# Last tokens as a ninth seven-product group, 64-key scores in 64x64 tiles, and new orders in a fused attention and gated-MLP kernel

## The chip, the cores and the metric

One core of a Trainium2 chip runs the kernel. The metric is the device time of one execution in microseconds; the comparison is between the kernel before and the kernel after the change, each run several times on the same chip. The engines are TensorE (PE, with its weight loads as PEld), VectorE (DVE), ScalarE (ACT), GpSimd (POOL) and SyncE (SP, which here only issues DMAs).

## The reference

Attention over 8 batch elements, 8 heads, 576 tokens and 64 features per head, with a bias that depends only on the distance of query and key, followed by a two-layer network with a sine gate on the 4608 tokens:

```python
scores = q @ k.T / 8 + bias_table[bucket(|i - j|)]        # T5 buckets, 32 of them
attn   = softmax(scores)
x      = (attn @ v), heads side by side                   # 4608 x 512
h      = x @ w_in                                         # 512 -> 2048
g      = h + sin(alpha * h)**2 / alpha
out    = g @ w_out                                        # 2048 -> 512, float32
```

## The kernel before

**Planning.** The kernel is a list of tasks with dependencies (`_graph`), each an emitting function of `_Ops` with an engine and a duration. `_Plan.run` walks through them with a small model of the chip; if `LINE` is given, the order of tasks on each engine is taken from that list of numbers and the model only gives start times, by which all engines' instructions are emitted. So the order of the work on PE, ACT, DVE, POOL and SP is written out, task by task, in `LINE`. `OPT` holds what else was chosen: which squares and copies run on ACT (`scalar`), which product pairs run in row halves (`rows`), the order of the POOL loads (`gq`).

**Attention.** Heads go in pairs (p = 0..3), one in each half of the 128 partitions. Keys lie on the output partitions of a score. `qk_t` (L1399, matmul L1405) scores 256 queries against 256 keys for a pair with four matmuls in two row halves of the array, 64 rows by 128 columns each; there are 16 such calls per element. `qk_tail` (L1385) takes the last 64 keys of two pairs against 512 queries, through `tail` (L1360): in the first two elements two 64x64 tiles on the diagonal (L1369), from the third element on one 128x128 matmul (L1364) with the block `kd`, in which `corners` (L1248, DVE) has put both heads' keys on the diagonal. `qk_s` (L1372) takes the last 64 keys against the last 64 queries in the same two ways, and `qk_r` (L1389, L1395) the first 512 keys against the last 64 queries. ACT takes the exponential of 1024 columns at a time (L1413, L1418), DVE multiplies the band near the diagonal by the exponentiated bias (L1441, L1423, L1427, L1383; the multipliers are `toep` and, made by POOL in `mask`, `mt`).

`av_w` (L1443) multiplies with v, for a pair p and a side w. For each group of 128 queries it issues one matmul of 130 columns for the last keys (L1451) and eight of 65 columns for the others (L1461); the 65th column gives the denominator. With w=0 there are two groups, with w=1 a third one for the last 64 queries, whose weights are 128 wide although 64 of the columns matter. `norm` (L1471, L1472) divides, and the result is turned either by PE and a copy (first element) or by a transposing DMA (`turn_x`) into `xT`, which holds four elements of 576 tokens.

**The network.** `moe_in` (L1498, matmul L1514) computes 128 rows of h for one block of tokens. The blocks `blk` are seven of 512 tokens, one of 448 and one of 576, cut where they cross the ring `xT` or a 512-column bank. Sine on ACT (`moe_sin`, L1522), square on ACT (L1527) or DVE (L1529), gate on DVE (`moe_g`, L1543).

The second layer works on groups of 512 tokens. For eight of them (`fast`) a 2x2 block product is made with seven block products instead of eight (`moe_fast`): `weight_sum` and `gate_sum` (L1578) make the sums on DVE, `products` (L1594, L1611) the products in 256-column matmuls into the PSUM banks X, Y and Z, `quarter` and `quarter_sum` (L1492/L1490, L1622) the results. Bank X holds products 1, 6, 7 and 4 in turn, each copied out before the next. The ninth group, the last 512 tokens, is multiplied directly: `moe_out` (L1547, L1558) with 512-column matmuls and `moe_half` (L1629, L1632) for its last 128 tokens.

**Row halves.** Changing how the array is divided costs PE time, so products may run "in rows": two products of a pair side by side, each on 64 rows of the contraction, first one half (turn 0), then, with halves swapped, the other (turn 1). `rows` names (pair number, f // 4). In `moe_fast` f // 4 is 0 or 1. Between the turns a DVE copy of one element of each bank (`touch_two`, L1587 and L1590) makes sure that both writes of a bank do not overlap.

**Loads.** q and k of the first elements come by POOL DMAs and are turned by PE (`turn`, L1340, on column halves of the array); later ones are staged in DRAM and turned by a transposing DMA. v comes by POOL DMAs (`load_v`, four per element, and `load_vt`, two per element for the last 64 keys). At the start `memsets` on DVE and `clear` on POOL write the constant parts.

Of the kernel before, what the change touches and what calls it, by code (L numbers as in the profile page):

```python
# [9 lines left out]
F16 = mybir.dt.float16  # L10
# [8 lines left out]
XR = 4 * S  # L19
# [82 lines left out]
class _Task:  # L102
    __slots__ = ("eng", "dur", "emit", "deps", "prio", "lat", "take", "seq", "sn", "name",
                 "m_in", "m_out", "pipe", "pkt", "flow", "start", "end", "idx", "got", "wait", "low", "alt",
                 "cold")

    def __init__(self, eng, dur, emit, deps=(), prio=0.0, lat=0.0, take=(), seq=None, name="",
                 mode=None, pipe=0.0, pkt=10, flow=False):
        self.pkt, self.flow = pkt, flow
        self.eng, self.dur, self.emit = eng, dur, emit  # L110
        self.deps = list(deps)
        self.prio, self.lat, self.take = prio, lat, list(take)
        self.seq, self.sn, self.name, self.pipe = seq, 0, name, pipe
        self.m_in, self.m_out = mode if isinstance(mode, tuple) else (mode, mode)
        self.start = self.end = None
        self.wait = 0.0
        self.low = 8
        self.cold = None
        self.alt = None
        self.got = []  # L120


class _Plan:
    HOP = 0.06
    LAT = {"PE": 0.17, "ACT": 0.1, "DVE": 0.09, "POOL": 0.1}
    SWITCH = {"PE": 0.096, "ACT": 1.3}
# [5 lines left out]
    STICK = 0.0  # L132

# [52 lines left out]
    def run(self):  # L186
# [21 lines left out]
        at = dict.fromkeys(line, 0)  # L208
        order = []
        while n:  # L210
            moved = False
            nxt = None
            for e, cand in pool.items():
# [4 lines left out]
                for t in cand:  # L218
# [6 lines left out]
                    for d in t.deps:  # L225
                        if d.eng != e or d.lat >= 1 or d.pipe:
                            x = d.end + self.HOP
                        else:
                            x = d.end + 0.025 if e == "DVE" else d.end - d.lat
                        if x > r:  # L230
                            r = x
                    r += t.wait
                    if t.pipe and e == "POOL" and len(self.segs[1]) >= self.OPEN:
# [50 lines left out]
                t.start = now  # L284
                free[e] = now + dur
# [1419 lines left out]
```

## Time and profile before

| | before |
|---|---|
| median of 3 runs | 373.88 us (373.77 to 374.48) |
| profiled execution: span | 370.6 us |
| instructions | 10525, of which 4379 matmuls and as many weight loads |
| busy PE, ACT, DVE, POOL | 356.4, 318.4, 318.8, 87.9 us |
| mean granted TensorE clock | 1.000 |

The span runs from the first to the last instruction of the profiled execution; the page gives no other time for that execution. A busy time is the time in which at least one instruction of the engine is in flight. For PE a matmul's own duration includes its drain, so the distance from one start to the next is what a matmul costs in a stream, not its duration. An idle time of an engine is put down to what ended it. In timeline rows the first column is the start, the second the time up to the end of the last instruction of the row; "x4" is the count; "64*128" is rows by columns of the array that are used.

### The profile page before, as it was taken

Reading aid. Unit: us, or ns where it says so; the run is one execution under the profiler, and the core shown is the slowest. Engines: PE = TensorE matmul, PEld = TensorE weight load, DVE = VectorE, ACT = ScalarE, POOL = GpSimd, SP = SyncE. Lnnn points to the kernel's source line nnn. Section 1 sums busy time; section 2 is a strip of 40 time slices with the busy share of each in tenths; the row PEclk is TensorE's granted clock in tenths of the full one; section 3 lists DMA queues with packets and bytes.
Section 4 is the critical chain, followed back from the end, with each engine's and each line's share of the span. In section 5 each row is a group of like instructions: output and inputs, shape, how many; then the busy total and the mean of one; then the engine's idle time right before and its main releaser. Section 6 shows DMA issues by size and latency. Waiting matters only on the chain.

```text
span 370.6 us, 10525 instructions
## 1 busy us (share of the span) xinstructions
PE 356.4 (96%) x4379; PEld 245.9 (66%) x4379; DVE 318.8 (86%) x711; ACT 318.4 (86%) x424; POOL 87.9 (24%) x105
## 2 busy tenths in 40 slices
PE   4969999999999999999999999999999999999996
PEld 3647546764666569755788987666965766745675
DVE  2679999999989998989998998899879997989733
ACT  5897999999999999999998999999899798476310
POOL 8895523085108000820050006200000000000000
PEclk9999999999999999999999999999999999999999
DMA  8999999899949954999799039907230012220014
GB/s 161 224 154 180 206 171 156 104 134 157 182 83 135 142 127 75 156 155 88 125 210 95 18 84 142 157 3 155 79 48 2 10 47 79 56 85 2 0 58 170
DMA packets 152415, 40.86 MB, mean 110 GB/s; under 512 B 134432, under 2 KB 151920, under 8 KB 152368
## 3 DMA queue, kind: packets, MB, share of 16 engines
q0 software_dynamic: 96656, 18.45, 60.2%
q1 hardware_dynamic: 55008, 21.22, 28.0%
q8 instruction: 34, 0.56, 0.6%
q10 hardware_dynamic: 704, 0.53, 0.6%
q14 instruction: 13, 0.11, 0.1%
HBM read 36.94 MB, written 15.93 MB: 143 GB/s over the span
## 4 chain that ended last, share of the span: by engine, by line
PE 87%; ACT 4%; POOL 3%; DMA 2%; DVE 2%; issue 1%; ACTq 0%; POOLq 0%; DVEq 0%
PE acc L1514 32%; PE acc L1611 26%; PE acc L1461 10%; PE acc L1405 9%; PE acc L1451 3%; PE acc L1558 3%; DMA wt<-in_k_dram 2%; PE acc L1364 2%; ACT s L1522 1%; PE acc L1395 1%; POOL mt L1292 1%; PE acc L1632 1%; DVE g L1543 1%; ACT u L1413 1%; POOL v L1219 1%
## 5 line engine op out<-in xcount | busy, mean ns | idle before, releaser
L1514 PE MATMUL acc<-xT,w_in 128*128 128x512 f16 (+3 forms) x704 | 134.2, 340 | 0.7 <-DVE g L1543 0.4
L1413 ACT ACTIVATE u<-acc 128x1024 f16<-128x1024 f32 x128 | 124.3, 1035 | 8.4 <-PE acc L1405 6.4
L1543 DVE SCALAR_TENSOR_TENSOR g<-s,inv_a,acc 128x512 f16<-128x512 f16 (+2 forms) x160 | 104.5, 691 | 8.6 <-ACT s L1527 6.5
L1522 ACT ACTIVATE s<-acc,alphaT 128x512 f16<-128x512 f32 (+2 forms) x144 | 93.2, 684 | 14.7 <-PE acc L1514 10.6
L1514 PEld LDWEIGHTS <-w_in 128*128 128x128 f16 x704 | 64.4, 98 | 55.8 <-DVE g L1543 1.8
L1611 PEld LDWEIGHTS <-g 128*128 128x128 f16 (+1 forms) x768 | 59.8, 96 | 18.0 <-issue 4.4
L1441 DVE TENSOR_TENSOR u<-u,toep 128x256 f16<-128x256 f16 (+1 forms) x128 | 59.4, 487 | 1.8 <-DMA toep<-e_sb 0.9
L1219 POOL DMA_DIRECT2D v<-in_v_dram x32 | 36.8, 1278 | 99.3 <-PE acc L1461 93.3
L1611 PE MATMUL acc<-w_out,g 128*128 128x256 f16 (+1 forms) x496 | 54.1, 271 | 0.0
L1405 PE MATMUL acc<-qT,kT 64*128 64x256 f16 x512 | 46.3, 279 | 3.9 <-DVE qT L1350 1.9
L1461 PE MATMUL acc<-v,u 128*128 128x65 f16 x1024 | 45.0, 193 | 0.1
L1527 ACT ACTIVATE s<-s 128x512 f16<-128x512 f16 (+2 forms) x67 | 41.4, 629 | 1.5
L1461 PEld LDWEIGHTS <-u 128*128 128x128 f16 x1024 | 40.6, 97 | 1.4 <-issue 0.5
L1611 PE MATMUL acc<-wt,g 128*128 128x256 f16 (+1 forms) x272 | 38.4, 272 | 0.0
L1611 PE MATMUL acc<-wt,sums 128*128 128x256 f16 (+1 forms) x272 | 34.6, 273 | 0.0
L1529 DVE TENSOR_TENSOR s<-s 128x512 f16<-128x512 f16 (+2 forms) x77 | 31.9, 422 | 2.6 <-ACT s L1522 2.3
L1472 DVE TENSOR_TENSOR xp<-acc,rden 128x256 f16<-128x256 f32 (+1 forms) x64 | 31.4, 491 | 2.2
L1405 PEld LDWEIGHTS <-kT 64*128 64x128 f16 x512 | 20.3, 96 | 16.1 <-issue 12.2
L1611 PEld LDWEIGHTS <-sums 128*128 128x128 f16 (+1 forms) x272 | 23.5, 97 | 7.9 <-issue 2.5
L1451 PE MATMUL acc<-vt,ut 128*128 128x130 f16 x128 | 28.3, 221 | 0.1
L1225 POOL DMA_DIRECT2D vt<-in_v_dram x16 | 14.1, 894 | 33.6 <-PE acc L1461 30.6
L1492 DVE COPY quarter<-acc 128x512 f32<-128x512 f32 x18 | 12.4, 687 | 9.3 <-PE acc L1611 4.7
(90 smaller groups left out, 361.6 us busy)
## 6 DMA issues: line engine op xcount, KB each, us to landing
out_dram<-quarter SPq DMA_DIRECT2D x32, 256.0 KB, 2.7
v<-in_v_dram POOLq DMA_DIRECT2D x32, 128.0 KB, 8.7
staged_k<-in_k_dram POOLq DMA_DIRECT2D x6, 576.0 KB, 10.8
staged_q<-in_q_dram POOLq DMA_DIRECT2D x5, 576.0 KB, 9.9
w_out<-in_moe_w_out_dram POOLq DMA_DIRECT2D x4, 512.0 KB, 8.7
w_in<-in_moe_w_in_dram POOLq DMA_DIRECT2D x4, 512.0 KB, 16.2
sums<-in_q_dram POOLq DMA_DIRECT2D x7, 144.0 KB, 5.6
out_dram<-outs SPq DMA_DIRECT2D x3, 256.0 KB, 2.0
```

Source lines behind the costliest of these rows:

```text
L1219: self.nc.gpsimd.dma_start(out=self.vs[t % 2][:, c, :, 0:D], in_=src)
L1405: self.nc.tensor.matmul(out=s[:, o:o + 256], lhsT=self.kT[t % 2][r, p, 128 * c:128 * c + 128], rhs=self.qT[t % 2][r, p, 256 * w:256 * w + ...
L1413: self.nc.scalar.activation(out=c["u"], in_=c["s"], func=AF.Exp, scale=0.125)
L1441: self.nc.vector.tensor_tensor(out=io, in0=io, in1=m, op=ALU.mult)
L1451: nc.tensor.matmul(out=c["av"][:, 130 * j:130 * j + 130], lhsT=tail, rhs=vt[:, p, :], start=True, stop=True, skip_group_check=True)
L1461: nc.tensor.matmul(out=c["av"][:, 130 * j + 65 * a:130 * j + 65 * a + 65], lhsT=l, rhs=vv[:, ch, 2 * p + a, 0:65], start=False, stop=True, ...
L1514: self.nc.tensor.matmul(out=c["h"][:, x:y], lhsT=self.w_in[:, j, 128 * f:128 * f + 128], rhs=self.xT[:, j, at:at + y - x], start=(j == 0 a ...
L1522: self.nc.scalar.activation(out=c["s"], in_=c["h"], func=AF.Sin, scale=self.alphaT[:, f:f + 1])
L1527: self.nc.scalar.activation(out=c["s"], in_=c["s"], func=AF.Square)
L1529: self.nc.vector.tensor_tensor(out=c["s"], in0=c["s"], in1=c["s"], op=ALU.mult)
L1543: self.nc.vector.scalar_tensor_tensor(out=o, in0=c["s"][:, x:y], scalar=self.inv_a[:, f:f + 1], in1=c["h"][:, x:y], op0=ALU.mult, op1=ALU.add)
L1611: self.nc.tensor.matmul(out=c[to][:, 256 * k:256 * k + 256], lhsT=a[r, 128 * k:128 * k + 128], rhs=b[r, :], start=to not in c["began"], st ...
```

## The change

What it does:

1. `blk` is nine blocks of 512. The last 64 tokens of all eight elements form a block of their own (`groups` number 8, the eighth in order, before the last element's 512). `xT` holds 512 tokens per element, a new `xt` all the tails. All nine groups go by seven products; `_blocks` of 448 and 576 tokens, `moe_out`, and `moe_half` are no longer used.
2. `av_w` makes two groups of 128 queries for either w; `av_tails` does the last 64 queries of all heads of an element in column halves of the array, `norm_tails` and `turn_tails` follow.
3. `tail` uses four 64x64 tiles for two head pairs in all elements; `kd`, `corners` and `clear` go; `load_vt` is four POOL DMAs per element; the constant memsets move to POOL.
4. `touch_two` goes. `half` lets PE wait for its own earlier matmul before the swapped half writes the bank. `rows` names 28 pieces.
5. The last group's product 3 gets a bank of its own (`W`), its product 4 is made and stored in two 256-column halves (`ending`).
6. New `LINE`, `scalar`, `gq` and rings (u tiles 14 for 12, x tiles 4 for 3); the model of the planner counts PE instructions and delays the start of a page of 256.

The diff, cut (the numbers of `LINE` and of `scalar` are left out):

```diff
-    blk=(512, 512, 512, 512, 512, 512, 512, 448, 576), fast=tuple(range(8)), split=True, no=2, nq=3, p_sum=0.1,
+    blk=(512, 512, 512, 512, 512, 512, 512, 512, 512),
+    groups=(0, 1, 2, 3, 4, 5, 6, 8, 7),
+    fast=(0, 1, 2, 3, 4, 5, 6, 7, 8),
...
-    rows=((0,2), (3,2), (4,2), (5,0), (5,1), (5,2), (5,3), (6,0), (6,1), (8,2), (9,0), (9,1),
-    (10,2), (11,2), (11,3), (12,2), (12,3), (13,0), (13,2), (15,0), (15,1), (15,2), (16,3),
-    (18,2), (20,3)), strict=False,
+    rows=((2, 0), (2, 1), (3, 0), (3, 1), (4, 0), (4, 1), (6, 0), (6, 1), (7, 0), (7, 1), (8,
+        0), (8, 1), (9, 0), (9, 1), (10, 0), (10, 1), (11, 1), (12, 0), (12, 1), (13, 1), (14, 0),
+        (14, 1), (15, 0), (15, 1), (16, 0), (16, 1), (18, 0), (18, 1)),
...
-    def tail(self, s, at, n, t, p, q0):
+    def tail(self, s, at, n, t, i, q0):
...
+        for b in range(2):
+            for a in range(2):
+                r, o = slice(64 * a, 64 * a + 64), 64 * (a ^ b)
+                self.nc.tensor.matmul(out=s[o:o + 64, 512 * b + at:512 * b + at + n],
+                                      lhsT=kT[r, 2 * i + b, 512:576], rhs=qT[r, 2 * i + b, q0:q0 + n],
+                                      start=True, stop=True)
...
+    def half(self, bank, at, n, lhsT, rhs, r, start):
+
+        was = None if start else self.wrote.get(bank)
+        if was is not None and was[0] != r and self.waited <= was[1]:
+            assert was[1] < self.marks, "no mark behind what the other half wrote"
+            hold = self.nc.tensor.nop(nofuse=True)
+            self.tc.add_manual_dep(hold.ins, self.at_mark[was[1]], SYNC, reason="rows")
+            self.waited = was[1] + 1
+        rows = slice(64 * r, 64 * r + 64)
+        self.last = self.nc.tensor.matmul(out=self.acc[:, bank, at:at + n], lhsT=lhsT[rows], rhs=rhs[rows],
+                                          start=start, stop=True, skip_group_check=True)
+        self.wrote[bank] = (r, self.marks)
...
+    def av_tails(self, c, bank, rs, t):
+
+        nc = self.nc
+        c["av"] = self.acc[:, bank, 0:260]
+        vv, vt, us = self.vs[t % 2], self.vt[t % 2], self.us[t % 2]
+        for i in range(2):
+            for b in range(2):
+                p, r = 2 * i + b, slice(64 * b, 64 * b + 64)
+                nc.tensor.matmul(out=c["av"][r, 130 * i:130 * i + 130], lhsT=us[:, 64 * p:64 * p + 64],
+                                 rhs=vt[:, p, :], start=not i, stop=True, skip_group_check=True)
+            for a in range(2):
+                for ch in range(4):
+                    for b in range(2):
+                        o, r = 512 * a + 256 * b + 64 * ch, slice(64 * b, 64 * b + 64)
+                        at = 130 * i + 65 * a
+                        nc.tensor.matmul(out=c["av"][r, at:at + 65], lhsT=rs[i]["u"][:, o:o + 64],
+                                         rhs=vv[:, ch, 4 * i + 2 * b + a, 0:65],
+                                         start=False, stop=True, skip_group_check=True)
...
-        T_v[t] += [gq(0.65, "load_vt", (t, a), deps=pre, pipe=0.27) for a in range(2)]
+        T_v[t] += [gq(0.6, "load_vt", (t, a, b), deps=pre, pipe=0.14) for a in range(2) for b in range(2)]
...
-        c22, q22 = finish(22, p7, zu, p5)
-        (p4, p3), all_c = group((4, 3), (ww(3), s_of(4)), ([c22], [q22]), ())
-        c12[1].deps.extend(p3)
-        finish(21, p4, None, [])
+        c22, q22, _ = finish(22, p7, zu, p5)
+        if i < 8:
+            (p4, p3), all_c = group((4, 3), (ww(3), s_of(4)), ([c22], [q22]), ())
+            c12[1].deps.extend(p3)
+            finish(21, p4, None, [])
+        else:
+            all_c = ending(cell, i, ww(3), s_of(4), c22, c12, xu)
...
+    def ending(cell, i, need4, need3, c22, c12, xu):
+
+        wu, p3 = [], []
+        for f in range(0, NF // 2, 2):
+            m = add("PE", 4 * 0.1092, None, prio=opt["p_mo"], mode="full", deps=need3(f) + p3[:1],
+                    name=f"mo{i}3.0.{f}", take=[] if p3 else [(1, wu)])
...
+        for k in range(2):
+            p4 = [add("PE", 4 * 0.1092, E("products", cell, i, (4,), f, 0, False, (k,), 4), prio=opt["p_mo"],
+                      mode="full", deps=need4(f) + [c22], name=f"mo{i}4.{k}.{f}") for f in range(0, NF // 2, 4)]
+            every += p4
+            cp = either(f"c21.{i}.{k}", 0.36, 0.38, lambda act, k=k: K.quarter_half(cell, k, act), deps=p4,
+                        prio=opt["p_ev"], take=[] if k else [(qr, ou)])
```

More of the change, by code (lines that the diff above doesn't have):

```diff
@@ L284, in run @@
                 t.start = now
+                if t.ins:
+                    for x in range(told // self.PAGE + 1, (told + t.ins) // self.PAGE + 1):
+                        pages.append(now + self.FETCH)
+                    told += t.ins
                 free[e] = now + dur
@@ L560, in later_loads @@
                     deps=[staged[t, kind]] + last_qk[t - 2])
-            if not kind:
-                e = add("DVE", 0.42, E("corners", t, range(NP)), deps=[c], prio=0.3)
-                e.wait = opt["late"]
-                T_c[t] = [e] * NP
             at[kind][t] = [c] * NP
@@ L748, in element @@
                     close(t, p, w, got)
+            if T_t[t] is None and all((t, x) in cells for x in (("R", 0), ("R", 1), ("S",))):
+                close_tails(t)
             yield
-        assert len(closed) == 2 * NP
+        assert len(closed) == 2 * NP and T_t[t] is not None
     BLK = _blocks(opt["blk"])
+    GROUPS = opt["groups"]
     NBLK = len(BLK)
@@ L838, in group @@
             turns = [[], []]
-            first = told = None
+            first = None
             for turn in range(2):
-                if turn:
-                    told = add("DVE", 0.18 if any(rows(f) for f in range(8)) else 0.0,
-                               lambda: any(rows(f) for f in range(8)) and K.touch_two(cell, names),
-                               deps=[m for m, r in turns[0] if r or opt["strict"]], prio=opt["p_touch"],
-                               name=f"told{pair}")
                 for f in range(0, NF // 2, 2):
@@ L937, in moe_out @@
                 break
-            if turn:
-                told = add("DVE", 0.12 if any(rows(f) for f in range(NF)) else 0.0,
-                           lambda: any(rows(f) for f in range(NF)) and K.touch(cell),
-                           deps=[m for m, r in turns[0] if r or opt["strict"]], prio=opt["p_touch"], name=f"told{pair}")
             for f in range(0, NF, 2):
@@ L1081 @@
+    n21 n22 n23 v2""".split(),)
 class _Ops:
@@ new lines, in full @@
+    def full(self, bank, at, n, lhsT, rhs, start):
+        if start:
+            self.wrote.pop(bank, None)
+        self.nc.tensor.matmul(out=self.acc[:, bank, at:at + n], lhsT=lhsT, rhs=rhs, start=start, stop=True,
+                              skip_group_check=True)
+    def half(self, bank, at, n, lhsT, rhs, r, start):
[9 more added lines that the diff above has]
+        self.wrote[bank] = (r, self.marks)
@@ L1441, in band_t, with av_w @@
         self.nc.vector.tensor_tensor(out=io, in0=io, in1=m, op=ALU.mult)
-    def av_w(self, c, bank, tiles, cr, ct, t, p, w):
+    def av_w(self, c, bank, tiles, ct, t, p, w):
         nc = self.nc
-        n = 3 if w else 2
-        c["av"] = self.acc[:, bank, 0:130 * n]
+        c["av"] = self.acc[:, bank, 0:260]
         vv, vt = self.vs[t % 2], self.vt[t % 2]
-        for j in range(n):
+        for j in range(2):
             o = 512 * (p % 2) + 256 * w + 128 * j
-            tail = ct["u"][:, o:o + 128] if j < 2 else self.us[t % 2][:, 64 * p:64 * p + 128]
-            nc.tensor.matmul(out=c["av"][:, 130 * j:130 * j + 130], lhsT=tail, rhs=vt[:, p, :],
-                             start=True, stop=True, skip_group_check=True)
+            nc.tensor.matmul(out=c["av"][:, 130 * j:130 * j + 130], lhsT=ct["u"][:, o:o + 128],
+                             rhs=vt[:, p, :], start=True, stop=True, skip_group_check=True)
@@ new lines, in turn_tails, with turn_tails_pe @@
+    def turn_tails(self, xcell, t):
+        self.nc.sync.dma_start_transpose(out=self.xt[:, t, :].rearrange("d (c s) -> d c s", c=2),
+                                         in_=xcell["x"][:, :])
+    def turn_tails_pe(self, xcell, cell, bank):
+        cell["o"] = o = self.acc[:, bank, :].bitcast(F16)
+        for i in range(2):
+            self.nc.tensor.transpose(out=o[:, 128 * i:128 * i + 128],
+                                     in_=xcell["x"][:, 128 * i:128 * i + 128], identity=self.ident[:, :])
@@ L1555, in moe_out @@
                     continue
-                r = slice(64 * (i ^ turn), 64 * (i ^ turn) + 64) if rows else slice(0, 128)
                 at = 128 * (tau % 4)
-                self.nc.tensor.matmul(out=c["mo"][i], lhsT=self.g[tau // 4][r, f, at:at + 128],
-                                      rhs=self.w_out[r, f, :], start=i not in c["began"],
-                                      stop=True, skip_group_check=True)
+                start = i not in c["began"]
                 c["began"].add(i)
+                args = (c["bank"][i], 0, DM, self.g[tau // 4][:, f, at:at + 128], self.w_out[:, f, :])
+                self.half(*args, i ^ turn, start) if rows else self.full(*args, start)
+        if rows and not turn:
+            self.mark()
     def weight_sum(self, i, k):
@@ L1608, in products @@
                         continue
-                    r = slice(64 * (x ^ turn), 64 * (x ^ turn) + 64) if rows else slice(0, 128)
-                    to, (a, b) = self.HOME[n], ab[n]
-                    self.nc.tensor.matmul(out=c[to][:, 256 * k:256 * k + 256],
-                                          lhsT=a[r, 128 * k:128 * k + 128], rhs=b[r, :],
-                                          start=to not in c["began"], stop=True, skip_group_check=True)
+                    to, (a, b) = "W" if n == 3 and "W" in c else self.HOME[n], ab[n]
+                    start = to not in c["began"]
                     c["began"].add(to)
+                    args = (c["bank"][to], 256 * k, 256, a[:, 128 * k:128 * k + 128], b)
+                    self.half(*args, x ^ turn, start) if rows else self.full(*args, start)
+        if rows and not turn:
+            self.mark()
     def quarter(self, c, what, act):
```

461 lines of the change are left out of this document (268 added, 193 removed), and 131 rows, old and new, of the table LINE.

## The prediction

> **What bounds it.** I read the page first (busy time, then the chain that ended last), then the busy time by stretches, then what TensorE waited for, then its timeline where the change bites.
>
> ```profile
> span 370.6 us, 10525 instructions
> PE 356.4 (96%) x4379; PEld 245.9 (66%) x4379; DVE 318.8 (86%) x711; ACT 318.4 (86%) x424; POOL 87.9 (24%) x105
> PE 87%; ACT 4%; POOL 3%; DMA 2%; DVE 2%; issue 1%; ACTq 0%; POOLq 0%; DVEq 0%
> 0.00:43.00 43.00, 32.71 (x624) 23.32 (x625) 30.27 (x84) 36.19 (x45) 34.51 (x56) 1.00 1.22 183
> 43.00:300.00 257.00, 256.70 (x3206) 178.59 (x3205) 237.34 (x523) 245.93 (x325) 53.36 (x49) 1.00 1.03 111
> 300.00:345.00 45.00, 44.48 (x375) 26.98 (x374) 39.37 (x85) 33.10 (x51) 0.00 (x0) 1.00 0.19 51
> 345.00:370.60 25.60, 22.46 (x179) 17.03 (x177) 11.80 (x22) 3.13 (x5) 0.00 (x0) 1.00 0.24 83
> ```
>
> The columns of the last four rows are the stretch, its length, then the busy time of PE, PEld, DVE, ACT and POOL. Three things are to be seen. From 43 us on PE is never out of work: 256.70 of 257 us, and the idle time at the end is the last copy and store. Second, 87% of the chain is PE's, so a microsecond of PE streaming taken out after 43 us is a microsecond of the kernel, as long as ACT and DVE keep up. Third, that condition is tight: in the long middle ACT is busy 245.93/257 = 95.7% and DVE 237.34/257 = 92.3%; only after 300 us have both room.
>
> The sum is made against this execution's span. The median of the runs shown, 373.88 us, lies 373.88 - 370.6 = 3.28 us above it; I hold that margin constant, so a microsecond of span is one of time. Less than 0.2% either way (0.75 us) counts as no change.
>
> **The 64-key scores in 64x64 tiles.** The 64 last keys of a head pair are scored at L1364 (from the third element on: a 128x128 block `kd` half zeros) and at L1369 (the first two elements: two 64x64 tiles).
>
> ```profile
> 273.45 0.59 PE L1364 MATMUL acc<-qT,kd 128*128 128x512 f16 x2
> 273.88 0.60 PE L1611 MATMUL acc<-wt,g 128*128 128x256 f16 x4
> 57.73 0.62 PE L1369 MATMUL acc<-qT,kT 64*64 64x512 f16 x4
> 58.28 1.48 PE L1611 MATMUL acc<-w_out,g 128*128 128x256 f16 x12
> 77.69 0.28 PE L1364 MATMUL acc<-qT,kd 128*128 128x64 f16 x4
> 77.80 0.60 PE L1611 MATMUL acc<-wt,sums 128*128 128x256 f16 x4
> ```
>
> Start to start is what counts (a row's own length includes its drain). Two full 512-column products take 273.88 - 273.45 = 0.43 us, 0.215 each. Four tiles on the diagonal take 0.55 us; less one change of mode (0.10, below) that is 0.45, two streams of 0.215, so tiles run two at a time. After the change the four matmuls of a call occupy four different quarters of the array. If all four run together, a call costs 0.215 instead of 0.43: 8 elements x 2 calls x 0.215 = **3.4 us** less. The last-query scores go from 0.11 (77.80 - 77.69) to about half: 8 x 0.05 = 0.4. Together **-3.8**. Bounds: -3.8 if four run at once; 0 if only pairs do, since four in pairs are again two streams. I take four, because the pieces are each in the trace: row halves side by side (next part) and column halves side by side (the transposes below).
>
> [...]
>
> **The last queries apart.** `av_w` for w=1 made three groups of nine matmuls, the third for 64 queries at a 128-wide price. It now makes two, and `av_tails` does all heads' last 64 queries of an element: 36 matmuls, in 18 pairs on the two column halves.
>
> ```profile
> 155.17 0.41 PE L1395 MATMUL acc<-qT,kT 64*128 64x64 f16 x16
> 155.41 0.38 PE L1405 MATMUL acc<-qT,kT 64*128 64x256 f16 x4
> 155.73 0.23 PE L1451 MATMUL acc<-vt,ut 128*128 128x130 f16 x1
> 155.80 0.41 PE L1461 MATMUL acc<-v,u 128*128 128x65 f16 x8
> 156.04 0.22 PE L1451 MATMUL acc<-vt,ut 128*128 128x130 f16 x1
> 156.09 0.41 PE L1461 MATMUL acc<-v,u 128*128 128x65 f16 x8
> 22.40 0.70 PE L1340 MATMUL acc<-ident,wt 96*64 96x96 f16 x24 [0.47 <-ACT u L1413]
> 23.03 0.31 PE L1369 MATMUL acc<-qT,kT 64*64 64x64 f16 x8
> ```
>
> A group of nine takes 156.04 - 155.73 = 0.31 (0.30 for the next, 33 ns a matmul). Removed: 32 x 0.30 = 9.6 us. The only column-tiled operation is the transposes: 24 in 0.63 us, less a mode change 0.53, 22 ns each or 44 a pair for 96 columns; two halves do run together. Added per element: 18 pairs at 33 ns = 0.60 (paced like the full groups) to 18 x 44 ns = 0.79 (paced like the transposes). I take 0.66, nearer the first because 65 columns stream in less than 96. 8 x 0.66 = 5.3. Net **-4.3** (-3.3 to -4.8).
>
> [...]
>
> **Output products and input matmuls.** The last 512 tokens took the direct way: at L1558 48 matmuls of 512 columns, at L1632 32 of 256.
>
> ```profile
> 341.03 0.86 PE acc L1558 x4
> 344.29 0.98 PE acc L1514 x8
> L1632 PE MATMUL acc<-w_out,g 128*128 128x256 f16 x32 | 4.5, 273 | 0.0
> L1514 PE MATMUL acc<-xT,w_in 128*128 128x512 f16 (+3 forms) x704 | 134.2, 340 | 0.7 <-DVE g L1543 0.4
> ```
>
> The chain gives 0.86/4 = 0.215 a 512-column matmul, so 48 x 0.215 + 32 x 0.109 = 13.8 us; seven products are 7 x 8 x 2 = 112 of 256 columns, 12.2. **-1.6**. Input: the same columns in 576 matmuls, not 704. Four of 576 columns in two pieces take 0.98, which is 0.215 x 576/512 x 4 = 0.97 and a hair: **-0.3**. Streaming in all: -3.8 - 4.3 - 1.6 - 0.3 = **-10.0 us**.
>
> **Mode changes.** 155.17 follows twelve 256-column products that started at 153.76 (12 x 0.109 = 1.31, so 155.07): a change full to row halves costs 0.10 us. In the timeline I count 162 such changes, 114 after 43 us, first and last:
>
> ```profile
> 57.42 0.38 PE L1514 MATMUL acc<-xT,w_in 128*128 128x512 f16 x1
> 57.73 0.62 PE L1369 MATMUL acc<-qT,kT 64*64 64x512 f16 x4
> 300.76 0.61 PE L1405 MATMUL acc<-qT,kT 64*128 64x256 f16 x8
> 301.30 0.93 PE L1514 MATMUL acc<-xT,w_in 128*128 128x448 f16 x4
> ```
>
> 110 of them enclose 55 visits to row halves. Seven of those visits hold products in row halves and gather about four scores each; the other 48 hold fewer than two. The `rows` list names 28 pieces instead of 9 that the code could use (entries with second number 2 or 3 never applied to products), so scores can be gathered behind products more often: I guess 55 visits become 35, -4.0 us (0 to -5.8, 26 left). Against it stand about 26 new visits: 12 for tails and 6 for last-query scores that used to be in full mode, 8 for `av_tails`, at 0.1 each where they touch another tiled visit and 0.2 where not: +2.6 to +5.2, taken 3.9. Net **0** (-3.2 to +5.2).
>
> **Waits.** The DVE touch between the two turns goes, and PE waits for its own earlier write instead.
>
> ```profile
> L1590 DVE COPY touched<-acc 1x1 f32<-1x1 f32 x6 | 0.6, 139 | 0.7 <-PE acc L1611 0.7
> L1587 DVE COPY touched<-acc 1x2 f32<-1x2 f32 x2 | 0.3, 144 | 0.3 <-PE acc L1611 0.3
> PE acc L1514 <- DVE g L1543: 0.4, 1, 0.4
> PE acc L1514 <- ACT u L1413: 0.2, 1, 0.2
> ```
>
> These are five pairs (three with two copies, two with one), and the only two PE waits after 43 us, in the last two rows, are for something else. Now 15 pairs have pieces in halves, each with one wait on PE's queue, behind which all matmuls stand, scores and so ACT's exponentials among them. A 256-column matmul lasts 273 ns where it streams 109, so an uncovered wait is about 0.17, a covered one nothing: 0 to 2.6, I take **+1.2**.
>
> **ACT and DVE.** Counted from the lists, 41 instead of 55 squares of the first seven blocks are ACT's: 14 x 0.632 = 8.8 us off ACT, 14 x 0.421 = 5.9 on DVE.
>
> ```profile
> L1527 ACT ACTIVATE s<-s 128x512 f16<-128x512 f16 x54 | 33.4, 632 | 1.1
> L1529 DVE TENSOR_TENSOR s<-s 128x512 f16<-128x512 f16 x58 | 23.9, 421 | 2.3 <-ACT s L1522 2.0
> L1254 DVE TENSOR_TENSOR kd<-kT 64x256 f16<-64x256 f16 x12 | 3.4, 284 | 0.4 <-DMA kT<-staged_k 0.3
> ```
>
> ACT's middle falls to 237; DVE's to 237.3 + 5.9 - 3.4 (corners) - 0.9 (touches) = 239. In a middle of about 250 us both are 95-96% busy, ACT as now, DVE tighter. Eight more gate sums (0.69 each) fall behind 300 us, where there is room. More than 250 to 240 can't be had. The last group's products share bank X through four copies; the third bank lets product 3 run under a copy (0.6-0.7 each). The front gets four small POOL loads of `vt` per element for two, while POOL is already 34.51 of 43 us busy there; DVE's memsets move onto POOL as `clear` leaves. Altogether new PE idle **+1.0** (-1 to +3); stores keep their last 256-column piece.
>
> **Sum:** -10.0 + 0 + 1.2 + 1.0 = -7.8: 373.9 - 7.8 = **366.1 us**.
>
> **Rivals.**
> *More gathered (12%).* All row visits merge and every wait is covered: -10.0 - 3.2 + 0 + 0.5 = -12.7, 361.2 us. For: the seven gathering visits. Against: ACT's 96%, which would leave it no slack.
> *ACT and DVE hold the middle, or tiles run in pairs only (20%).* If the middle doesn't get below 253, only 4 of its some 7 us are kept, and with the -1.6 and -0.3 behind 300 us and the waits the time is about 370. Pairs only: -7.8 + 3.8 = -4.0, 369.9. Against: both kinds of halves overlap in rows above. [...]
> *Nothing (4%).* Order gains and extra mode changes (+5.2), waits (2.6) and idle (2) cancel streaming: 373.7.
> *Slower: weight loads of the column halves don't overlap (9%).* Place: `av_tails`.
>
> ```profile
> L1340 PEld LDWEIGHTS <-sums 96*64 96x64 f16 x120 | 4.3, 142 | 2.1 <-issue 1.2 <-DMA sums<-in_k_dram 0.8
> L1340 PEld LDWEIGHTS <-wt 96*64 96x64 f16 x96 | 2.7, 116 | 1.5 <-issue 1.0 <-DMA wt<-in_q_dram 0.2
> L1461 PEld LDWEIGHTS <-u 128*128 128x128 f16 x1024 | 40.6, 97 | 1.4 <-issue 0.5
> ```
>
> A 64-wide load in column halves lasts 116 to 142 ns, 19 to 45 longer than a full one. If that came on top of each matmul's 33 ns, a visit would be 36 x 52 = 1.9 us, or with 78 ns 2.8, and eight of them 15.0 to 22.5 in place of 9.6: 366.1 + (15.0 - 5.3) = 375.8, up to 383. It decides from (5.3 + 7.8)/8 = 1.6 us a visit on. Against: with the very loads of 116 ns the transposes ran at 22 ns a matmul. [...]
>
> **Chances and range.** Forecast (363 to 369) 55%, the others as named: faster 0.87, same 0.04, slower 0.09. The range, 362 to 371, leaves out the best of the first rival and the slower ones.
>
> **What will show it.** L1364's successor: four 512-column tiles in about 0.22 us plus mode changes (0.43 refutes). A column-half visit of 36 in 0.60-0.79 us. Fewer than 114 mode changes after 43 us, or as many. PE idle in the middle under 2 us; ACT about 237 us of it. A wait of PE on itself beyond 0.2 us, or a middle over 254 us, would make the prediction wrong.

## The result, and the profile after

| | before | after |
|---|---|---|
| median | 374.18 us (4 runs, 373.77 to 374.52) | 367.69 us (4 runs, 367.27 to 368.35) |
| ratio | 1 | 0.9829, 95% interval 0.9813 to 0.9844 |
| profiled execution | 370.6 us span | 365.5 us span, 367.27 us time |

The forecast was 366.1 us in a range of 362 to 371. The kernel is faster by 6.5 us where 7.8 were expected.

The page of the kernel after, its span, busy times and shares of the chain:

```profile
span 365.5 us, 11027 instructions
...
PE 350.9 (96%) x4633; PEld 241.3 (66%) x4633; DVE 318.5 (87%) x694; ACT 311.2 (85%) x420; POOL 99.3 (27%) x139
...
PE 81%; DVE 7%; ACT 3%; DMA 3%; POOL 3%; issue 2%; POOLq 0%
```

The busy time by stretches of the same kernel (stretch, length, then PE, PEld, DVE, ACT, POOL, and the granted clock):

```profile
0.00:43.00 43.00, 34.83 (x609) 24.84 (x610) 28.47 (x73) 32.28 (x44) 32.99 (x72) 0.88 1.21 170
43.00:300.00 257.00, 254.22 (x3505) 172.61 (x3503) 236.21 (x523) 244.80 (x321) 63.82 (x64) 1.00 1.02 114
300.00:345.00 45.00, 45.00 (x376) 29.61 (x375) 40.41 (x81) 28.00 (x46) 0.62 (x1) 1.00 0.13 36
345.00:365.50 20.50, 16.87 (x149) 14.27 (x146) 13.38 (x21) 6.10 (x11) 1.82 (x3) 1.00 0.35 103
```

PE still sets the time, but 2.78 of the middle's 257 us are now idle, where it was 0.30 before: PE has begun to run into ACT and, once, into DVE. What it waited for, after 43 us (who, for whom: total us, times, longest):

```profile
PE acc L1520 <- ACT u L1535: 1.4, 4, 0.4
PE acc L1571 <- ACT u L1535: 0.5, 1, 0.5
PE acc L1478 <- ACT quarter L1643: 0.5, 1, 0.5
PE acc L1478 <- DVE quarter L1645: 0.2, 1, 0.2
```

Five waits are for an exponential (L1535), two for the copies of a quarter: one at 206.95 us (L1645), one in the last group at 361.74 us (L1643). PE's timeline of the changed kernel, where its new operations follow each other:

```profile
111.15 0.61 PE L1490 MATMUL acc<-wt,sums 64*128 64x256 f16 x8
111.70 0.41 PE L1470 MATMUL acc<-qT,kT 64*64 64x512 f16 x4
112.04 0.25 PE L1589 MATMUL acc<-vt,us 128*64 128x130 f16 x2
112.12 0.42 PE L1596 MATMUL acc<-v,ur 128*64 128x65 f16 x16
112.37 0.22 PE L1589 MATMUL acc<-vt,us 128*64 128x130 f16 x2
112.43 0.42 PE L1596 MATMUL acc<-v,ur 128*64 128x65 f16 x16
112.78 0.41 PE L1520 MATMUL acc<-qT,kT 64*128 64x64 f16 x16
...
222.99 0.63 PE L1470 MATMUL acc<-qT,kT 64*64 64x512 f16 x8
223.55 0.23 PE L1571 MATMUL acc<-vt,ut 128*128 128x130 f16 x1
```

Eight products in row halves stream 4 x 0.109 = 0.44 of the first 0.55 us; 0.11 is the change of mode behind them. The tile call takes 0.34 to the next start. Two calls in a row, at 222.99 us, take 0.56, so a call more costs 0.22, one stream of 512 columns, and the change behind it is the other 0.12. The visit of `av_tails`, 36 matmuls, takes 112.78 - 112.04 = 0.74, less a change 0.62.

### The profile page after: what moved, and what is told of

It reads as the page before. It is cut to its first block, busy times and chain, and to the rows that moved or that the text cites. A ratio compares the mean times of both kernels' runs of the same rounds, so it can differ in the third digit from the quotient of the medians.

```text
span 365.5 us, 11027 instructions
## 1 busy us (share of the span) xinstructions
PE 350.9 (96%) x4633; PEld 241.3 (66%) x4633; DVE 318.5 (87%) x694; ACT 311.2 (85%) x420; POOL 99.3 (27%) x139
## 4 chain that ended last, share of the span: by engine, by line
PE 81%; DVE 7%; ACT 3%; DMA 3%; POOL 3%; issue 2%; POOLq 0%
PE acc L1662 30%; PE acc L1478 15%; PE acc L1490 13%; PE acc L1576 9%; PE acc L1520 7%; PE acc L1571 3%; DVE g L1688 3%; DMA wt<-in_q_dram 2%; ACT u L1535 2%; PE acc L1470 2%; DMA wt<-in_k_dram 1%; DVE s L1674 1%; POOL sums L1330 1%; PE acc L1596 1%; DVE u L1563 1%
## 5 line engine op out<-in xcount | busy, mean ns | idle before, releaser
L1535 ACT ACTIVATE u<-acc 128x1024 f16<-128x1024 f32 x128 | 121.3, 1054 | 8.7 <-PE acc L1520 8.2
L1662 PE MATMUL acc<-xT,w_in 128*128 128x512 f16 x512 | 116.1, 379 | 0.0
L1667 ACT ACTIVATE s<-acc,alphaT 128x512 f16<-128x512 f32 x144 | 92.4, 684 | 19.5 <-PE acc L1662 18.5
L1688 DVE SCALAR_TENSOR_TENSOR g<-s,inv_a,acc 128x512 f16<-128x512 f16 x144 | 102.4, 743 | 2.8 <-ACT s L1672 1.4
L1563 DVE TENSOR_TENSOR u<-u,toep 128x1024 f16<-128x1024 f16 (+1 forms) x128 | 58.2, 487 | 2.6 <-DMA toep<-e_sb 1.2
L1520 PE MATMUL acc<-qT,kT 64*128 64x256 f16 (+1 forms) x768 | 55.2, 253 | 3.0 <-ACT u L1535 2.2
L1478 PEld LDWEIGHTS <-g 128*128 128x128 f16 x416 | 39.9, 98 | 14.1 <-issue 3.2
L1674 DVE TENSOR_TENSOR s<-s 128x512 f16<-128x512 f16 x83 | 33.7, 420 | 10.9 <-ACT s L1667 10.9
L1490 PE MATMUL acc<-w_out,g 64*128 64x256 f16 x496 | 41.0, 269 | 0.1
L1672 ACT ACTIVATE s<-s 128x512 f16<-128x512 f16 x61 | 37.1, 627 | 0.9
L1478 PE MATMUL acc<-wt,g 128*128 128x256 f16 x232 | 30.6, 273 | 0.7 <-ACT quarter L1643 0.5
```

Source lines behind the costliest of these rows:

```text
L1478: self.nc.tensor.matmul(out=self.acc[:, bank, at:at + n], lhsT=lhsT, rhs=rhs, start=start, stop=True, skip_group_check=True)
L1490: self.last = self.nc.tensor.matmul(out=self.acc[:, bank, at:at + n], lhsT=lhsT[rows], rhs=rhs[rows], start=start, stop=True, skip_group_c ...
L1520: self.nc.tensor.matmul(out=s[:, 512 * a + o:512 * a + o + n], lhsT=kT[r, p, 128 * c:128 * c + 128], rhs=qT[r, p, q0:q0 + n], start=True, ...
L1535: self.nc.scalar.activation(out=c["u"], in_=c["s"], func=AF.Exp, scale=0.125)
L1563: self.nc.vector.tensor_tensor(out=io, in0=io, in1=m, op=ALU.mult)
L1662: self.nc.tensor.matmul(out=c["h"], lhsT=self.w_in[:, j, 128 * f:128 * f + 128], rhs=x, start=j == 0, stop=j == 3, skip_group_check=True)
```

## The experiments

Times are medians; "over after" is the difference to 367.69 us, ratios are to the kernel before on the same chip.

**The kernel before again, unchanged, for a second trace.**

> The kernel before, unchanged, to see its own time beside its span. The prediction held the margin between the two at 3.28 us (373.88 - 370.6). The changed kernel shows 367.27 beside a span of 365.5, a margin of 1.77. Theory A: the margin is about 1.8 us in both kernels, and the profiled execution of before was one of some 372.4 us or its span was off; then spans of before come out near 372. Theory B: the margin of before really is about 3.3, so 1.4 of the 6.5 us gained lie outside the span.

374.18 us; ratio 1.000 (0.9988 to 1.0011). Its page, and its middle:

```profile
span 372.0 us, 10525 instructions
...
43.00:300.00 257.00, 256.41 (x3200) 177.96 (x3200) 237.38 (x524) 245.83 (x325) 53.28 (x49) 1.00 1.03 112
```

This execution took 374.17 us, 2.17 more than its span; for the kernel after it is 367.27 - 365.5 = 1.77. The span of 370.6 on which the prediction was built was a short one, so the margin of 3.28 was too large: other executions of this kernel with spans of 370.2 to 370.4 us took 372.3 to 372.6. With this trace the part from 43 us to PE's last matmul can be set out. Streaming is every matmul's columns at 0.417 ns and 2.3 ns more each, which is 0.216 us for 512 and 0.109 for 256 (the kernel after has 23 matmuls of 512 columns in 4.96 us from 334.73 us on, and 20 of 256 in 2.18 us from 332.33 us on); halves at one half and quarters at one quarter, but the tiles on the diagonal of the kernel before, which ran two at a time, at one half too. A change is taken at 0.105 us, between the 0.10 of the prediction's row and the 0.11 above; "rest" is what remains:

| 43 us to PE's end, us | before | after | difference |
|---|---|---|---|
| wall time | 325.92 | 319.34 | -6.6 |
| streaming | 309.4 | 296.7 | -12.6 |
| mode changes, 118 and 131 | 12.4 | 13.8 | +1.4 |
| PE waits | 0.6 | 2.6 | +2.0 |
| rest | 3.6 | 6.3 | +2.7 |

Over the whole run streaming falls by 10.6 us, from 328.8 to 318.2; the other 2.0 are done before 43 us now (1.1 against the first trace of before).

**Pairs in place of four tiles.** The second head's keys stay in the same column half as the first's, so that the four tiles of a call lie on the diagonal; such tiles took two streams before the change (0.45 us, as in the prediction).

```diff
-                r, o = slice(64 * a, 64 * a + 64), 64 * (a ^ b)
+                r, o = slice(64 * a, 64 * a + 64), 64 * a
```

(with the last keys' v, ones and multipliers laid out to match).

> The changed kernel with the four 64x64 tiles of a 64-key call on the diagonal only (both head pairs alike, with mask and v laid out to match), so that just two tiles can run at a time. Theory A (four at once): a visit of four 512-column tiles goes from 0.34 us back to 0.55, 16 x 0.215 + 8 x 0.05 = +3.8 us of PE, about 371.5, less what falls into the 2.6 us of PE idle. Rival B (tiles already run in pairs): no change, 367.7.

370.26 us, 2.6 over after; ratio 0.9896 (0.9879 to 0.9913). PE's timeline of this kernel at the same call:

```profile
112.65 0.62 PE L1470 MATMUL acc<-qT,kT 64*64 64x512 f16 x4
113.19 0.25 PE L1589 MATMUL acc<-vt,us 128*64 128x130 f16 x2
```

0.34 has become 0.54: one more stream of 512 columns, 0.20. Sixteen calls of 0.20 make 3.2 us and the last-query calls a few tenths. 2.6 us reach the time; about 1.0 falls in the front, before 43 us, where PE does not set the end. So four tiles do run at once, by 0.34 against 0.54. In the changed kernel the two row halves then write one bank at the same time, into different halves of its partitions (rows 0 to 63 into partitions 0 to 63 and rows 64 to 127 into 64 to 127, crosswise in the other bank).

**Column halves one after the other.** The loops of `av_tails` change order: all 18 matmuls of half 0, then those of half 1.

```diff
-        for i in range(2):
-            for b in range(2):
+        for b in range(2):
+            for i in range(2):
...
-            for a in range(2):
-                for ch in range(4):
-                    for b in range(2):
+                for a in range(2):
+                    for ch in range(4):
```

> The changed kernel with the 36 matmuls for the last 64 queries issued one column half after the other, instead of alternating. Theory A (the halves overlap, weight loads included): a visit goes from 0.64 us and a mode change to about 36 x 0.033 = 1.19, 8 x 0.55 = +4.4 us, about 372. Rival B (a visit is held by something the two halves share, the issue or the load of weights): a visit stays within 0.1 us and the kernel within 1 us. Rival C (a column half alone loads its weights slower than 33 ns a matmul): more than 1.3 us a visit.

371.48 us, 3.8 over after; ratio 0.9926 (0.9900 to 0.9952). First and last row of one visit, and the one behind it, in PE's timeline of this kernel:

```profile
73.50 0.24 PE L1589 MATMUL acc<-vt,us 128*64 128x130 f16 x1
...
74.42 0.41 PE L1595 MATMUL acc<-v,ur 128*64 128x65 f16 x8
74.77 0.25 PE L1470 MATMUL acc<-qT,kT 64*64 64x64 f16 x8
```

The visit is 1.27 us instead of 0.74; 8 x 0.53 = 4.2. Less a change of 0.12 it is 1.15, or 32 ns a matmul in one half alone: the pace of the full array's groups (33 in the prediction's rows). Two halves together run at 0.62/36 = 17 ns a matmul. Matmuls and weight loads of the two halves overlap: 36 loads of 109 to 111 ns each (L1589, L1596 in the kernel after) go with the 36 matmuls of those 0.62 us. The slower rival needed the opposite.

**No products in row halves.**

```diff
-    rows=((2, 0), (2, 1), (3, 0), (3, 1), (4, 0), (4, 1), (6, 0), (6, 1), (7, 0), (7, 1), (8,
...
+    rows=(),
```

> The changed kernel with an empty rows list: all products in full mode, no waits of PE on itself, the same order of tasks. Counted along the order of PE's tasks, the mode changes rise from 159 to 265. Theory A (a mode change costs 0.10 us whoever stands behind it, a wait on itself 0.17): +106 x 0.10 - 15 x 0.17 = +8.0 us, about 375.7. Rival B (the waits and the doubled matmul count of the halves eat what they save): within 1 us of the changed kernel, 367 to 369.

387.04 us, 19.4 over after; ratio 1.0343 (1.0287 to 1.0399). This is far beyond the expected 8. After 43 us there are 237 mode changes, 106 more, or 11.1 us; PE's waits are 9.9 us, 7.3 more. PE's largest wait, and a stretch of ten us, of this kernel:

```profile
PE acc L1518 <- ACT u L1533: 4.7, 6, 2.4
```

```profile
210.00:220.00 10.00, 7.57 (x53) 4.63 (x51) 7.69 (x13) 6.76 (x8) 0.00 (x0) 0.83 2.11 183
```

The changes are what was priced. The other 8 us I put down to the order, which was written for products in rows and now brings scores late: in the stretch shown ACT is busy 6.76 of 10 us, and PE, which waits for it in turn, 7.57 at a clock of 0.83. That the order does this was not tried apart. So rows are worth about 11 us of changes in this order. The run cannot tell what the longer list alone added over the old one.

**A wait at every second turn.** 56 pieces of `products` get a wait on PE's last matmul.

```diff
+        if rows and turn:
+            hold = self.nc.tensor.nop(nofuse=True)
+            self.tc.add_manual_dep(hold.ins, self.last.ins.name, SYNC, reason="rows")
```

> The changed kernel with a wait of PE on its own newest product in row halves ahead of each of the 56 second-turn pieces, not only ahead of the first of a pair. 19 of the 56 stand right behind such a product, with nothing between. Theory A (a wait with a score between costs nothing, one without costs 0.17 to 0.33, as at the one such place in the changed kernel): 19 x 0.17 to 0.33 = +3.2 to +6.3 us, 371 to 374. Rival B (all 56 cost 0.17): +7 to +9.5. Rival C (such waits are free): 367.7.

374.10 us, 6.4 over after; ratio 1.0018 (0.9999 to 1.0037): such waits alone can eat the whole gain. In the accounting above the rest rises by 6.0 and PE's waits by 0.8. In 19 of the 56 places the piece of the first turn stands directly ahead; 6.0 us over these 19 are 0.32 each, and one of them is in PE's timeline of this kernel, where 16 half matmuls take 1.20 us from start to start (114.75 to 115.95) for a stream of 0.87. The other 37, with a score or other work between, cost nothing to be seen. In the changed kernel there is one place of the first kind among the 15:

```profile
254.33 0.61 PE L1490 MATMUL acc<-w_out,g 64*128 64x256 f16 x8
255.10 0.61 PE L1490 MATMUL acc<-w_out,g 64*128 64x256 f16 x8
```

0.77 us from start to start where eight half matmuls stream 0.44: 0.33 for one uncovered wait. Its name is not among PE's waits above, since the time hides in the distance between starts.

**Four casts moved from DVE to ACT in the front.**

```diff
-    scalar=frozenset("""c11.1 c11.2 c11.3
+    scalar=frozenset("""cast00 cast10 cast01 cast11 c11.1 c11.2 c11.3
```

> The changed kernel with the first four casts on ACT again, as before the change. PE then begins some 1.2 us later (4.95 in the profile before, 3.79 in the changed one). By the accounts of the two traces about 1.6 us more PE work is done in the first 43 us after the change. Theory A (that comes from the earlier start): +1.0 to +1.2 us, 368.8. Rival B (the loads of the next heads set the front's pace, the casts have slack): within 0.4 us, 367.7.

367.84 us; ratio 0.9851 (0.9823 to 0.9878), whose interval overlaps that of the change. No difference: the casts have slack. (By the table above the more work before 43 us is 2.0 us, not 1.6.)

**PE filled in the front.** In the front of the kernel after, PE's granted clock drops:

```profile
20.00:30.00 10.00, 8.27 (x136) 6.72 (x133) 8.79 (x23) 7.47 (x9) 9.64 (x19) 0.53 1.14 110
```

```profile
27.23 0.30 PE L1571 MATMUL acc<-vt,ut 128*128 128x130 f16 x1
...
27.78 0.30 PE L1571 MATMUL acc<-vt,ut 128*128 128x130 f16 x1
```

(a stretch, then PE's timeline: a group of nine takes 0.55 us there in place of 0.30). The experiment puts 32 matmuls on constants, whose results nobody reads, into that stretch.

```diff
-FILLS = ()
+FILLS = ((22, 5), (24, 5), (27, 9), (32, 8), (35, 3), (39, 2))
```

> The changed kernel with 32 added matmuls of 256 columns on constants, into banks that are free, put where PE stood idle between 14 and 26 us. In the changed kernel's trace the granted clock falls to 0.50 from 21 to 30 us and a group of nine matmuls takes 0.55 us instead of 0.30. Theory A (PE is the bound there from 25 us on, and the low clock comes from the idle time before it): eight groups at 0.25 and some scores come back, -2 to -3 us, about 365.2. Rival B (the front waits for ACT and the loads anyway): 367.2 to 367.7 although the clock stays up. Rival C (that little work doesn't keep the clock up): the drop stays and the time too.

371.40 us, 3.7 over after; ratio 0.9944 (0.9922 to 0.9965). The mean clock from 20 to 30 us rose to 0.84, and yet PE came to the first last-query scores behind `av_tails` at 37.99 us, where the kernel after is there at 38.01:

```profile
37.99 0.20 PE L1520 MATMUL acc<-qT,kT 64*128 64x64 f16 x2
40.03 0.38 PE L1520 MATMUL acc<-qT,kT 64*128 64x64 f16 x14 [1.83 <-issue]
```

```profile
38.01 0.41 PE L1520 MATMUL acc<-qT,kT 64*128 64x64 f16 x16
38.35 1.04 PE L1662 MATMUL acc<-xT,w_in 128*128 128x512 f16 x4
```

(the filled kernel first, then the kernel after). The filled kernel alone can't show whether the low clock costs the front time, since its fills are some 3.5 us of PE work themselves (32 x 0.109). The traces without fills say more. The granted clock is 0.50 for 10.2 us in the kernel after, whose mean is 0.986; the means of 0.991 with pairs and of 0.981 with the halves one after the other make it some 6.6 and 14 us there (estimated: what is lacking to 1, over spans of 368.8 and 370.3 us, at 0.50). PE begins the first `av_tails` at 37.51 us with pairs, at 37.29 in the kernel after and at 38.13 with the halves one after the other. Twice as long at that clock goes with 0.6 us. So the low clock is at most a small part of the front's length. What sets it was not traced; POOL is busy 9.64 of the 10 us shown. What cost the filled kernel its time is new: a stop of 1.83 us in the middle of 16 equal matmuls, put down to "issue", that is, to nothing that the profile shows. The kernel after and those with pairs and with the halves one after the other have no such stop in their timelines.

**The same number of instructions, somewhere else.** 32 or 64 matmuls of 32 by 32 on constants go into the start of the kernel, so that later instructions have higher numbers on PE's queue; and 32 into the kernel before.

```diff
+            if not i:
+                self.shift(32)
...
+    def shift(self, n):
+        ones = self.ap(self.vs[0], 64, [[66, 32]])
+        for _ in range(n):
+            self.nc.tensor.matmul(out=self.acc[0:32, 7, 0:32], lhsT=ones, rhs=ones, start=True, stop=True)
```

(64 in the second of them.)

> The changed kernel with 32 tiny matmuls (64 instructions) on constants ahead of the first work of PE, from about 1 us, where PE is idle until 3.8. Nothing else differs; every later PE instruction stands 64 places further on. The 64 instructions of the fill run came with a stop of 1.83 us at 38 us that the trace puts down to no other engine. [...] Rival B (the stop came from the fills themselves or their place): 367.3 to 368.

> As the run with 32 tiny matmuls, with 64 (128 instructions). [...]

> The kernel before with the same 32 tiny matmuls (64 instructions) ahead of PE's first work. In the changed kernel this brought a stop of 1.8 us near 38 us and 3.5 us in all. [...]

With 32 matmuls, that is 64 instructions with their loads, the kernel after takes 371.17 us, 3.5 over after (0.9911, 0.9882 to 0.9941); with 64 matmuls 369.12, 1.4 over (0.9869, 0.9841 to 0.9897). The kernel before with 32 takes 374.08 (1.0001, 0.9984 to 1.0019). The stop in PE's timeline of the kernel with 32, and then two of its stretches (PE and PEld columns up to the stop, and the clock in the last stretch of the front):

```profile
39.43 0.38 PE L1527 MATMUL acc<-qT,kT 64*128 64x64 f16 x14 [1.81 <-issue]
```

```profile
0.00:38.50 38.50, 31.88 (x605) 24.19 (x606) 25.98 (x67) 27.98 (x38) 29.55 (x66) 0.91 1.15 169
...
30.00:43.00 13.00, 11.19 (x245) 7.80 (x241) 8.81 (x33) 9.38 (x15) 7.60 (x11) 0.88 1.37 191
```

The same of the kernel with 64:

```profile
38.23 0.38 PE L1603 MATMUL acc<-v,ur 128*64 128x65 f16 x12 [1.32 <-issue]
```

```profile
0.00:37.50 37.50, 32.91 (x605) 25.62 (x606) 25.21 (x65) 27.70 (x38) 28.32 (x65) 0.91 1.15 167
...
30.00:43.00 13.00, 11.68 (x251) 8.34 (x248) 9.33 (x34) 10.01 (x17) 6.17 (x10) 1.00 1.33 191
```

And the stretch up to the stop of the filled kernel, shown above:

```profile
0.00:39.00 39.00, 31.52 (x605) 23.44 (x606) 26.25 (x66) 27.94 (x38) 29.12 (x66) 0.96 1.15 166
```

Three kernels stop at three different places of the work and at the same count, 605 matmuls and 606 loads. The stop belongs to a place in PE's instruction stream and not to an operation. Behind the stop of 1.32 us the clock stayed at 1.00, and 1.4 us were lost; behind that of 1.81 the clock fell to a mean of 0.88 over 13 us, which is 12% of 13 or 1.6 us more, and 3.5 were lost. (In the filled kernel the clock fell as well, to a mean of 0.89 from 30 to 43 us.) Up to 38.1 us the kernel after has begun fewer:

```profile
0.00:38.10 38.10, 29.93 (x577) 22.46 (x579) 25.08 (x65) 27.66 (x38) 28.29 (x65) 0.87 1.16 168
```

In it the same count comes 28 matmuls later, behind 38.35 us and so among input matmuls of 0.215 us, and nothing stands still there. The shipped order thus avoids a loss of 1.4 to 3.5 us that these shifts bring about; the kernel before did not notice its shift. That the planner's counting of PE instructions found this order is argued, since it wasn't tried by itself, and no run shows the pages of its model.

**Without the written orders.** In either kernel the planner makes its own order.

```diff
-    line=_line(LINE),
+    line=(),
```

> The changed kernel without its written order: each engine takes the ready task of the highest priority, by the planner's model. 226 mode changes instead of 159. Theory A (the written order carries much of the time, and the change of the work its 6 to 10 us): far slower than 367.7, by 20 us or more, and to be compared with the kernel before without its order, which should then be slower than this by 6 to 12 us. Rival B (the gain came from searching the order again): without orders the changed kernel is no faster than the one before.

> The kernel before without its written order, by the planner's priorities, for comparison with the changed kernel without its order (449.8 us). 214 mode changes instead of 158. Theory A (the change of the work is worth its 6 to 12 us under any order): 456 to 462. Rival B (the gain came from the new search): 450 or less.

One run each: the changed kernel 449.8 us, the kernel before 433.07. Of two kernels left to the planner the changed one is slower by 16.7 us, though it has less to stream: the sign that rival B named, both times. The mean granted clocks are 0.935 and 0.968, and what is lacking to 1 makes 29 us of the one span and 14 of the other (estimated: 0.065 x 447.8 and 0.032 x 431.3, if PE set the pace throughout), so the lower clock can hold most of the difference. The runs show that shorter streaming alone does not become time; it takes an order that keeps PE busy. They do not show what the new order is worth by itself: an order searched anew for the kernel before, which might also take less than 374 us, was not tried.

The ninth group by seven products and the third bank were not tried alone. No run beat the kernel after.

## Why the prediction was right, and where it was off

- **The bound.** Right: from 43 us on PE sets the time, and what left its stream left the time, as far as other engines kept up.
- **64-key scores, -3.8.** Right: 0.34 with a change, and pairs cost 0.20 more a call. The rival "in pairs only" is out.
- **The last queries apart, -4.3.** Right, a little better: 0.62 a visit for 0.66 makes -4.6. The rival of loads that do not overlap is out: even one half after the other is 1.15 us, below the 1.6 from which it would have decided.
- **Streaming in all, -10.0.** By the matmuls of the two traces, at the prices above, -10.6 over the run. The ninth group's -1.6 and the input's -0.3 are in that count and were not tried alone.
- **"Mode changes", net 0.** This is the step that failed. I guessed that 55 visits to row halves would become 35; there are 54. Scores did gather: of 125 calls of `qk_t` and `qk_r` after 43 us 86 stand in a visit with products, where it was 34 of 115 (second trace of before), and visits of scores alone fell from 49 to 27. But the visits with products rose from 8 (I had counted seven) to 27, because the order scatters the pieces, and the sum had nothing for those. With the visits for tails and `av_tails` there are 131 changes for 118, +1.4 us. I had read from the list what only the order decides.
- **"Waits", +1.2.** The mechanism is real, and its price was set too low: an uncovered wait costs 0.32, not 0.17. By my own sign, a wait of PE on itself beyond 0.2, the prediction would have been wrong; but 14 of 15 are covered, so the term is 0.3.
- **"ACT and DVE", +1.0.** Too small. PE's waits grew by 2.0. Beside them the rest grew by 2.7: five more waits with a drain of about 0.17 each (estimated from the 273 ns that a matmul of 109 lasts) make 0.9, the uncovered wait 0.3; about 1.5 stays unassigned. PE is idle for 2.78 us of the middle where under 2 was to show it. ACT's load is not where this went wrong. In 250 us from 43 us on, the middle that I expected, ACT is busy 237.83 us, and 237 was forecast:

```profile
43.00:66.00 23.00, 21.06 (x206) 11.81 (x203) 22.79 (x48) 22.94 (x32) 8.89 (x10) 1.00 1.53 171
43.00:293.00 250.00, 247.22 (x3407) 166.88 (x3406) 229.87 (x512) 237.83 (x314) 63.82 (x64) 1.00 1.04 115
```

  The waits stand in one place: four of the five for an exponential, 1.6 of 1.9 us, fall between 59 and 64 us, where ACT has no slack (22.94 of 23 us), and the long rest of the middle has 0.3. What changed there is in ACT's exponentials and squares from 43 to 300 us, before (second trace) and after:

```profile
L1413 ACT ACTIVATE u<-acc 128x1024 f16<-128x1024 f32 x99 | 95.7, 1028 | 4.5 <-PE acc L1405 3.8
```

```profile
L1535 ACT ACTIVATE u<-acc 128x1024 f16<-128x1024 f32 x112 | 105.9, 1056 | 2.9 <-PE acc L1520 2.5
...
L1672 ACT ACTIVATE s<-s 128x512 f16<-128x512 f16 x42 | 25.6, 627 | 0.6
```

  The squares went as counted, 54 to 42, -7.7 us. But 13 more of these exponentials fall into that stretch, +10.2: the new order does 16 instead of 26 before 43 us, and none instead of 4 from 300 us on (one of them over the edge). ACT was as full from 43 to 66 us before, 22.72 of 23 us (first trace). That the ten left over from the front are what PE now waits for near 60 us is a guess that was not tried.
- **The sum.** Beside the forecast, mode changes, waits and the rest cost 3.9 us more (1.4 + 2.0 + 2.7, less the 1.2 and 1.0 forecast); against that streaming gave 0.6 more, and 2.0 us more of it were done in the front. So the gain is 6.5 for 7.8. That it is no further off is partly luck. The rest of the way from 366.1 to 367.69 is the median of before, 374.18 here for 373.88. The margin of 3.28 was wrong too, but it drops out of a difference that is taken from the median.

## What to carry to other kernels

Tiles and column halves are worth what their parts in an old trace say, if the operations that show them overlapping are there: price them per call from start to start and here they came out within 6% (0.22 for 0.215, 0.62 for 0.66). Count the visits to another array mode in the order that will run and not in the list that allows it: what gathers scores also opens visits of its own. Look for the stretch in which the second engine has no slack, not only for its share of the whole. When PE's short matmuls become denser, try a shift of its instruction numbers too: one small insertion can show how much of a result hangs on the places in its stream (here 1.4 to 3.5 us).

## What the runs showed of the hardware that was not expected

- PE stops for 1.3 to 1.8 us without a cause in the profile, in three kernels at the same count of its instructions, 605 matmuls and 606 loads, each time among matmuls of 64 to 130 columns (1.83, 1.81 and 1.32 us). In the kernel after, where input matmuls of 0.215 us stand at that count, nothing stops. What makes PE stop was not seen.
- A stop can cost more than its length: behind 1.81 us of it the clock fell to a mean of 0.88 over 13 us, and 3.5 us were lost; behind 1.32 us it stayed at 1.00, and 1.4 were lost.
- A PE wait on PE's own last matmul costs 0.32 us if nothing stands between (6.0 us over 19 places; 0.33 at the one in the kernel after), and nothing to be seen behind as little as one score call.
- Alternating column halves of the array issue a matmul, mostly of 65 columns, every 17 ns on average, one half alone every 32.
- PE's clock fell to a mean of 0.53 for ten us in the front although PE was 83% busy there, and where it was low for some 14 instead of 6.6 us (estimated above) PE came 0.6 us later to the first `av_tails`. With 32 matmuls added there the mean was 0.84; why it falls was not settled.
